# Attention and two expert layers: the first add of a pair's exponentials goes to VectorE, and the first batch is divided earlier

## The chip, the cores and the metric

The kernel runs on one core of a Trainium2 chip. Its time is the device time in microseconds of one execution, and the median of several runs is what is compared. The profile is of one execution; its span runs from the first instruction to the last.

## What is computed

Three layers over 4 batches of 448 positions: capped attention with 12 heads, a sparse layer of 4 attention experts of which the two best count for each position, and a gated feed-forward layer.

```python
def _attn_ref(q, k, v, cap):
    scores = scale * np.matmul(q, k.transpose(0, 1, 3, 2))
    scores = cap * np.tanh(scores / cap)
    attn = np.exp(scores - np.max(scores, axis=-1, keepdims=True))
    attn = attn / (np.sum(attn, axis=-1, keepdims=True) + 1e-09)
    return np.matmul(attn, v)
...
def _moe_ref(x, w_gate, wq, wk, wv, wo):
    logits = x @ w_gate
    topk = np.argpartition(-logits, 2, axis=-1)[..., :2]
...
    for e in range(E):
        a = causal softmax of scale * (x @ wq[e]) @ (x @ wk[e]).T
        ye = a @ (x @ wv[e]) @ wo[e]
        out += (e is in topk) * w[e] * ye
...
def _moe2_ref(x, w_in, g_ln, w_sg, b_sg, w_out):
    u, v = halves of gelu(x @ w_in)
    return x + (u * (w_sg @ layer_norm(v) * g_ln + b_sg)) @ w_out
```

## The kernel before

The heads are taken two at a time: 6 pairs for each of 4 batches, 24 pairs, and pair i is worked on in `slot(i)`. A slot computes the scores transposed, with 112 keys on the partitions, in two halves (h = 0 and 1) of two key chunks each. For a half, TensorE makes the scores s, ScalarE a tanh of each chunk and one exponential over both, which leaves p. The sum over keys that the softmax needs is built in two steps: the four chunks of p are added into one tile pb, and matmuls with a one-hot matrix (`sums`, on TensorE) add up its partitions for two pairs at once. pb takes three adds: the first joins the two chunks of half 0, the other two add the chunks of half 1 (`add_up`, on VectorE, at the end of the slot). For batch 0 the first add is VectorE's, for the 18 pairs of the other batches GpSimd's. `values` multiplies the previous pair's p by v and stores the product in os.

The rest of the program is laid into these slots at named places: "a" (twice: after the scores of half 0, and after the values; the second is "a1" to `normed`), "w" (before the values), "p" (after the scores of half 1) and "n" (the end). In slots 0 to 9 `prepare_weights` converts a 64-bit weight in 12 steps (wi0 to wi11, VectorE) and multiplies it (w2ps). `normed` finishes a batch six slots after its pairs: `invert` takes the reciprocal rs of the sums and sends it through DRAM (rd) into tiles rb that repeat it over the partitions; `over_sums` multiplies os by rb, in three parts; `in_parts` splits each part into a rounded part xh and a rest xl. From xh and xl the expert layer starts, by a plan: for a batch whose pairs end with slot 5, `queries_keys` (qk) comes in slots 10, 11, 14 and 15 of the program, `weigh` (scores a, their negated maxima m on VectorE, called minima here, exponentials pe on ScalarE) in slots 12, 13, 16 and 17, `values_chunk` (v, lg) in slots 12 and 13, `settle` (GpSimd scales pe by cs, 8 instructions) and `turn` (TensorE transposes pe into tr, copied out of PSUM to pt by VectorE) in slots 14, 15, 18 and 19; each later batch six slots later. At "p" the transposes are mixed into the matmuls of qk or v. All of these share three PSUM buffers g. `w_out` converts another weight (wuw, wum) on VectorE and then on GpSimd, at the end of slots 14 and 20 among others.

Up to slot 24 every engine executes in the order in which the code is written; a TensorE matmul is also tied to the one before it. DMAs are issued by SyncE in that order too. After slot 24 (near 290 us) a scheduler that estimates times sets the order. Every instruction of ScalarE, VectorE and GpSimd carries the line of one helper, L104, and every matmul L119, so rows are told apart by the tile names.

Of the kernel before, what the change touches and what calls it, by code (L numbers as in the profile page):

```python
# [10 lines left out]
F32 = mybir.dt.float32  # L11
# [6 lines left out]
ALU = mybir.AluOpType  # L18
# [3 lines left out]
B, H, S, D = 4, 12, 448, 64  # L22
# [6 lines left out]
CP, NC = 112, 4  # L29
# [8 lines left out]
def drain(gen):  # L38
    for _ in gen:
        pass  # L40
# [32 lines left out]
def build(ctx: ExitStack, tc: tile.TileContext, a: dict):  # L73
# [4 lines left out]
    def rnd(eng, out, in_):  # L78

        if eng == "a":  # L80
            act.activation(out, in_, AF.Copy)
        elif eng == "v":
            dve.tensor_copy(out, in_)
        else:
            pool_e.tensor_scalar(out, in_, 1.0, 0.0, op0=ALU.mult, op1=ALU.add)

    def rest(eng, out, in_, hi):

        e = dve if eng == "v" else pool_e
        e.tensor_tensor(out, in_, hi.bitcast(F32), op=ALU.subtract)  # L90
# [17 lines left out]
    act, dve, pool_e = InOrder(nc.scalar), InOrder(nc.vector), InOrder(nc.gpsimd)  # L108

    def pin(ins):  # L110

        if pe_pin[0] and pe_last:
            tc.add_manual_dep(ins.ins, pe_last[0].name,
                              mybir.DependencyInfo(mybir.DependencyClass.NoSync, mybir.DependencyReason.DATA),
                              reason="order")
        pe_last[:] = [ins.ins]

    def mm(*args, **kw):
        pin(nc.tensor.matmul(*args, **kw))  # L119
# [9 lines left out]
    onehot = const.tile([CP, 3, 32], F32, name="onehot")  # L129
# [44 lines left out]
    at = ah.enter_context(tc.tile_pool(name="at", bufs=2, side="right"))  # L174
    ps_s = ah.enter_context(tc.tile_pool(name="ps_s", bufs=2, space=PSUM, side="right"))
    ps_o = ah.enter_context(tc.tile_pool(name="ps_o", bufs=1, space=PSUM, side="right"))
    os_t, sums_t, pend, rb_d = {}, {}, {}, {}

    def load_pair(b, hp):

        qp = at.tile([128, S], F32, tag="qp", name=f"qp{b}_{hp}", bufs=3)
        kp = at.tile([128, S], F32, tag="kp", name=f"kp{b}_{hp}", bufs=3)
        vv = at.tile([CP, 2, NC, D], F32, tag="vv", name=f"vv{b}_{hp}", bufs=3)
        nc.sync.dma_start(kp, a["kT"][b, :, hp, :])
        nc.sync.dma_start(qp, a["qT"][b, :, hp, :])
        if (b, hp) == pairs[0]:
            scale()
            load_w(0)
        nc.sync.dma_start(vv, a["v"][b, :, 2 * hp:2 * hp + 2])
        return qp, kp, vv  # L190

    def scores(b, hp, h, qp, kp):

        p = at.tile([CP, 2, 2, S], F32, tag="p", name=f"p{b}_{hp}_{h}", bufs=4)
        for c2 in range(2):
            c = 2 * h + c2
            s = ps_s.tile([128, 2, 512], F32, tag="s", name=f"s{b}_{hp}_{c}")
            for j in range(2):
                r = slice(64 * j, 64 * j + 64)
                mm(s[:CP, j, :S], kp[r, c * CP:(c + 1) * CP], qp[r, :], start=True, stop=True)  # L200
            act.activation(p[:, :, c2, :], s[:CP, :, :S], AF.Tanh, scale=tsc[:CP])
            yield 805.0


        act.activation(p, p, AF.Exp, scale=capt[:CP])
        if h == 0:
            pb = at.tile([128, 2, S], F32, tag="pb", name=f"pb{b}_{hp}", bufs=3)[:CP]
            (dve if b == 0 else pool_e).tensor_tensor(pb, p[:, :, 0, :], p[:, :, 1, :], op=ALU.add)
            pend[b, hp] = (p, pb)
        else:  # L210
            p0, pb = pend[b, hp]
            pend[b, hp] = (p0, p, pb)

    def add_up(b, hp):
        _, p, pb = pend[b, hp]
        for c2 in range(2):
            dve.tensor_tensor(pb, pb, p[:, :, c2, :], op=ALU.add)

    def values(b, hp, vv):
        po = ps_o.tile([128, 512], F32, tag="po", name=f"po{b}_{hp}")  # L220
        for c in range(NC):
            for j in range(2):
                mm(po[64 * j:64 * j + 64, :S], vv[:, j, c, :], pend[b, hp][c // 2][:, j, c % 2, :],
                                 start=(c == 0), stop=(c == NC - 1))
            yield 805.0
        if hp % 2 == 0:
            os_t[b, hp // 2] = ao.tile([128, 2, S], F32, tag="os", name=f"os{b}_{hp}", bufs=5)
        act.activation(os_t[b, hp // 2][:, hp % 2, :], po[:, :S], AF.Copy)

    def sums(b, i):  # L230
        g = ps_g.tile([128, 512], F32, tag="g", name=f"sum{b}_{i}")
        for j in range(4):
            mm(g[32 * j:32 * j + 32, :S], onehot[:, i, :], pend[b, 2 * i + j // 2][2][:, j % 2, :],
                             start=True, stop=True)
        if i == 0:
            sums_t[b] = ao.tile([128, S], F32, name=f"rs{b}", tag="rs", bufs=1)
            dve.tensor_copy(sums_t[b], g[:, :S])
        else:
            dve.tensor_tensor(sums_t[b], sums_t[b], g[:, :S], op=ALU.add)
        yield 870.0  # L240

    def invert(b):
        dve.reciprocal(sums_t[b], sums_t[b])
        d = dr.tile([4, 32, S], F32, tag="rd", name=f"rd{b}")
        nc.sync.dma_start(d.rearrange("j r s -> (j r) s"), sums_t[b])
        rb_d[b] = d
        for h2 in range(2):
            load_rb(b, h2)

    pairs = [(b, hp) for b in range(B) for hp in range(HP)]  # L250
    ld = {}

    def slot(i, side):

        if i == 0:
            ld[0] = load_pair(*pairs[0])
            ld[1] = load_pair(*pairs[1])
        if i + 2 < len(pairs):  # L260
            qk = [at.tile([128, S], F32, tag=t, name=f"{t}{i + 2}", bufs=3) for t in ("qp", "kp")]
            b, hp = pairs[i + 2]
            nc.sync.dma_start(qk[1], a["kT"][b, :, hp, :])
            nc.sync.dma_start(qk[0], a["qT"][b, :, hp, :])
            ld[i + 2] = qk
        if i < len(pairs):
            first = scores(*pairs[i], 0, *ld[i][:2])
            drain(islice(first, 2))
            side("a")
            drain(first)  # L270
        else:
            side("a")
        side("w")
        if i:
            b, hp = pairs[i - 1]
            drain(values(b, hp, ld.pop(i - 1)[2]))
        if 0 < i < len(pairs) - 1:
            b, hp = pairs[i + 1]
            vv = at.tile([CP, 2, NC, D], F32, tag="vv", name=f"vv{b}_{hp}", bufs=3)
            nc.sync.dma_start(vv, a["v"][b, :, 2 * hp:2 * hp + 2])  # L280
            ld[i + 1] = (*ld[i + 1], vv)
        side("a")
        if i < len(pairs):
            drain(scores(*pairs[i], 1, *ld[i][:2]))
        side("p")
        if i:
            b, hp = pairs[i - 1]
            if hp % 2 == 1:
                drain(sums(b, hp // 2))
        if i < len(pairs):  # L290
            add_up(*pairs[i])
        side("n")


# [10 lines left out]
    def over_sums(b, h2):  # L305
        x = os_t[b, h2]
        dve.tensor_mul(x, x, rbs.pop((b, h2)))

    def in_parts(b, h2):

        if h2 == 0:
            X[b] = (xp.tile([128, KC, S], F32R, tag="xh", name=f"xh{b}"),
                    xp.tile([128, KC, S], F32R, tag="xl", name=f"xl{b}"))
        (xh, xl), x, o = X[b], os_t.pop((b, h2)), slice(2 * h2, 2 * h2 + 2)
        rnd("v", xh[:, o, :], x)
        rest("v", xl[:, o, :], x, xh[:, o, :])

    def normed(n, place):

        b = (n - 1) // HP - 1  # L320
        step = (n % HP, place)
        if n > B * HP + 4 or b < 0:
            return
        if step == (1, "a1"):
            invert(b)
        elif step == (3, "w"):
            over_sums(b, 0)
            over_sums(b, 1)
            load_rb(b, 2)
        elif b == 0 and step == (3, "a1"):  # L330
            in_parts(b, 0)
            in_parts(b, 1)
        elif step == (4, "w"):
            if b:
                in_parts(b, 0)
            over_sums(b, 2)
            if not b:
                in_parts(b, 2)
        elif b and step == (4, "a1"):
            in_parts(b, 1)  # L340
            in_parts(b, 2)
# [296 lines left out]
    with tc.tile_pool(name="pre", bufs=2) as pre:  # L638
        if WARM:
# [3 lines left out]
            g = ps_g.tile([128, 512], F32, tag="g", name="warm")  # L643
# [9 lines left out]
    for n in range(PRE_SLOTS, B * HP + 1):  # L653
        slot(n, beside(n))
# [256 lines left out]
```

## Time and profile before

| | us |
|---|---|
| median of 3 runs | 558.57 |
| lowest and highest | 557.87, 561.39 |
| the profiled execution | 559.72 |
| its span | 558.0 |
| TensorE busy | 532.7 |
| VectorE busy | 361.4 |
| ScalarE busy | 325.7 |
| GpSimd busy | 141.4 |

The span is the profiled execution without what lies around it. A busy time adds up an engine's instructions; TensorE's are pipelined, so its figure says that it had work and not that it ran at its peak. What limits the time at a place is told by the waits and by the timeline of that place.

### The profile page before, as it was taken

How to read it: one execution, taken by the hardware profiler on the slowest of the kernel's cores; microseconds unless marked ns; L12 is line 12 of the kernel's file. 1: busy time of each engine (PE TensorE's matmuls, PEld its weight loads, DVE VectorE, ACT ScalarE, POOL GpSimd, SP SyncE). 2: the span in 40 equal slices, each digit the busy share in tenths (PEclk: the TensorE clock that was granted, in tenths of full speed). 3: DMA queues.
4: the chain of work that ended last, by engine and by line, in shares of the span. 5: the costliest groups of instructions: out<-in, count | busy, mean ns of one | idle time of the engine just before them, and what ended most of it. 6: DMA issues, size and time to landing. Idle time of an engine off the chain costs nothing.

```text
span 558.0 us, 7562 instructions
## 1 busy us (share of the span) xinstructions
PE 532.7 (95%) x2732; PEld 346.3 (62%) x2732; DVE 361.4 (65%) x725; ACT 325.7 (58%) x508; POOL 141.4 (25%) x180
## 2 busy tenths in 40 slices
PE   7999999899999989999988989999999989999997
PEld 2333333455555554656557655878768879889996
DVE  3899999984666636567567599676631786485300
ACT  5988888688687896577822345353534344253211
POOL 0000122141155251243340364515521131031000
PEclk9999999999999999999999978999999999999999
DMA  8974615752424141322056221010421000000111
GB/s 246 338 217 123 207 51 160 223 175 80 130 67 142 50 140 49 103 71 67 22 158 165 54 59 58 29 58 0 162 101 64 2 0 34 33 34 33 51 49 66
DMA packets 30596, 53.97 MB, mean 97 GB/s; under 512 B 3872, under 2 KB 22880, under 8 KB 30560
## 3 DMA queue, kind: packets, MB, share of 16 engines
q1 hardware_dynamic: 29408, 48.26, 28.2%
q0 software_dynamic: 1152, 5.24, 2.8%
q8 instruction: 21, 0.34, 0.3%
q14 instruction: 15, 0.12, 0.1%
HBM read 41.83 MB, written 11.67 MB: 96 GB/s over the span
## 4 chain that ended last, share of the span: by engine, by line
PE 73%; DVE 16%; ACT 6%; DMA 2%; issue 2%; POOL 1%; DVEq 0%; POOLq 0%; ACTq 0%; SPq 0%
PE o L119 15%; PE po L119 10%; PE s L119 10%; PE qk L119 8%; PE sp L119 7%; PE v L119 5%; ACT p L104 4%; PE a L119 3%; PE hv L119 3%; PE hu L119 3%; PE w2ps L119 2%; PE tr L461 2%; PE av L119 2%; DVE pb L104 2%; DVE rs L104 2%
## 5 line engine op out<-in xcount | busy, mean ns | idle before, releaser
L104 ACT ACTIVATE p<-s,tsc 112x896 f32<-112x896 f32 x96 | 91.4, 1005 | 24.4 <-PE s L119 24.4
L119 PE MATMUL s<-qp,kp 64*112 64x448 f32 x384 | 84.4, 557 | 3.4 <-ACT p L104 3.4
L104 ACT ACTIVATE p<-p,capt 112x1792 f32<-112x1792 f32 x48 | 85.9, 1790 | 1.3
L104 POOL TENSOR_TENSOR pb<-p 112x896 f32<-112x896 f32 x18 | 38.9, 2163 | 166.6 <-ACT p L104 96.9
L119 PE MATMUL po<-p,vv 112*64 112x448 f32 x384 | 77.3, 545 | 0.0
L104 DVE TENSOR_TENSOR pb<-pb,p 112x896 f32<-112x896 f32 x48 | 57.3, 1194 | 16.0 <-ACT p L104 12.3
L119 PEld LDWEIGHTS s<-qp,kp 64*112 64x112 f32 x384 | 30.8, 172 | 50.6 <-issue 21.3
L119 PEld LDWEIGHTS po<-p,vv 112*64 112x64 f32 x384 | 25.5, 136 | 45.0 <-issue 44.0
L104 ACT ACTIVATE pe<-a,m 112x112 f32<-112x112 f32 (+3 forms) x64 | 31.2, 491 | 25.3 <-DVE m L104 24.5
L104 POOL TENSOR_SCALAR pe<-pe,cs 112x112 f32<-112x112 f32 (+1 forms) x64 | 31.6, 519 | 50.3 <-DVE cs L104 50.2
L104 DVE CUSTOM_DVE_ANT_0 a<-a,neg 112x112 f32<-112x112 f32 (+3 forms) x64 | 27.7, 464 | 20.0 <-PE a L119 20.0
L119 PE MATMUL qk<-xh,wqk_h 128*128 128x448 f32 x96 | 38.2, 398 | 2.6 <-DVE xh L104 2.6
L119 PE MATMUL o<-gh,wu_h 128*128 128x448 f32 x96 | 35.6, 371 | 0.8 <-DMA wu_h<-wud 0.8
L119 PE MATMUL o<-gl,wu_h 128*128 128x448 f32 x96 | 35.6, 371 | 0.0
L119 PE MATMUL qk<-xh,wqk_l 128*128 128x448 f32 x96 | 35.4, 369 | 0.0
L119 PE MATMUL a<-qk 64*112 64x112 f32 (+3 forms) x128 | 29.9, 440 | 5.6 <-ACT pe L104 3.4
L119 PE MATMUL o<-gh,wu_l 128*128 128x448 f32 x96 | 35.0, 370 | 0.0
L104 ACT ACTIVATE ob<-o 128x448 f32<-128x448 f32 x24 | 13.0, 541 | 31.5 <-PE o L119 31.3
L119 PE MATMUL v<-wvg_h,xh 128*112 128x260 f32 x96 | 28.7, 299 | 0.7 <-ACT pe L104 0.7
L461 PE MATMUL tr<-ident,pe 112*112 112x112 f32 x160 | 23.7, 261 | 4.9 <-DVE lg L104 1.8
L119 PE MATMUL v<-wvg_h,xl 128*112 128x260 f32 x96 | 27.1, 283 | 0.0
L119 PE MATMUL v<-wvg_l,xh 128*112 128x260 f32 x96 | 27.1, 282 | 0.0
(226 smaller groups left out, 1096.5 us busy)
## 6 DMA issues: line engine op xcount, KB each, us to landing
kp<-in_kT_dram SPq DMA_DIRECT2D x24, 224.0 KB, 3.1
qp<-in_qT_dram SPq DMA_DIRECT2D x24, 224.0 KB, 3.2
vv<-in_v_dram SPq DMA_DIRECT2D x24, 224.0 KB, 3.1
rb<-rd SPq DMA_DIRECT2D x24, 224.0 KB, 4.7
out_dram<-ob SPq DMA_DIRECT2D x24, 224.0 KB, 1.9
wuw<-in_w_out_dram SPq DMA_DIRECT2D x8, 384.0 KB, 3.5
wud<-wuw SPq DMA_DIRECT2D x16, 192.0 KB, 1.9
ws<-in_wqk_dram SPq DMA_DIRECT2D x4, 384.0 KB, 6.0
```

The costliest lines, as they stand in the source:

```text
L104: ins = f(*args, **kw)
L119: pin(nc.tensor.matmul(*args, **kw))
L461: pin(nc.tensor.transpose(g[:CP, j * CP:(j + 1) * CP], pe[:, j * CP:(j + 1) * CP], ident))
```

## The change

The first add of every pair, of batch 0 too, becomes a VectorE instruction, and it is issued at another place: no longer right behind the exponentials of half 0, but behind the second place "a" (the second minima, and what `normed` does at "a1") and before the scores of half 1. `add_up` gets the half as an argument; the tile pb is made there, and the sums find it in `pbs`. For batch 0 the steps of `normed` move: the first two divisions and the load of the third rb from slot 9 "w" to slot 8 "a1", the splitting of these parts from slot 9 "a1" to slot 9 "w", and the third part's division and splitting from slot 10 "w" to slot 9 "n".

```diff
--- before.py
+++ after.py
@@ -174,7 +174,7 @@
     at = ah.enter_context(tc.tile_pool(name="at", bufs=2, side="right"))
     ps_s = ah.enter_context(tc.tile_pool(name="ps_s", bufs=2, space=PSUM, side="right"))
     ps_o = ah.enter_context(tc.tile_pool(name="ps_o", bufs=1, space=PSUM, side="right"))
-    os_t, sums_t, pend, rb_d = {}, {}, {}, {}
+    os_t, sums_t, pend, pbs, rb_d = {}, {}, {}, {}, {}
 
     def load_pair(b, hp):
 
@@ -204,15 +204,17 @@
 
         act.activation(p, p, AF.Exp, scale=capt[:CP])
         if h == 0:
-            pb = at.tile([128, 2, S], F32, tag="pb", name=f"pb{b}_{hp}", bufs=3)[:CP]
-            (dve if b == 0 else pool_e).tensor_tensor(pb, p[:, :, 0, :], p[:, :, 1, :], op=ALU.add)
-            pend[b, hp] = (p, pb)
+            pend[b, hp] = (p,)
         else:
-            p0, pb = pend[b, hp]
-            pend[b, hp] = (p0, p, pb)
-
-    def add_up(b, hp):
-        _, p, pb = pend[b, hp]
+            pend[b, hp] = (*pend[b, hp], p)
+
+    def add_up(b, hp, h):
+        p = pend[b, hp][h]
+        if h == 0:
+            pb = pbs[b, hp] = at.tile([128, 2, S], F32, tag="pb", name=f"pb{b}_{hp}", bufs=3)[:CP]
+            dve.tensor_tensor(pb, p[:, :, 0, :], p[:, :, 1, :], op=ALU.add)
+            return
+        pb = pbs[b, hp]
         for c2 in range(2):
             dve.tensor_tensor(pb, pb, p[:, :, c2, :], op=ALU.add)
 
@@ -230,7 +232,7 @@
     def sums(b, i):
         g = ps_g.tile([128, 512], F32, tag="g", name=f"sum{b}_{i}")
         for j in range(4):
-            mm(g[32 * j:32 * j + 32, :S], onehot[:, i, :], pend[b, 2 * i + j // 2][2][:, j % 2, :],
+            mm(g[32 * j:32 * j + 32, :S], onehot[:, i, :], pbs[b, 2 * i + j // 2][:, j % 2, :],
                              start=True, stop=True)
         if i == 0:
             sums_t[b] = ao.tile([128, S], F32, name=f"rs{b}", tag="rs", bufs=1)
@@ -281,6 +283,7 @@
             ld[i + 1] = (*ld[i + 1], vv)
         side("a")
         if i < len(pairs):
+            add_up(*pairs[i], 0)
             drain(scores(*pairs[i], 1, *ld[i][:2]))
         side("p")
         if i:
@@ -288,7 +291,7 @@
             if hp % 2 == 1:
                 drain(sums(b, hp // 2))
         if i < len(pairs):
-            add_up(*pairs[i])
+            add_up(*pairs[i], 1)
         side("n")
 
 
@@ -323,19 +326,19 @@
             return
         if step == (1, "a1"):
             invert(b)
-        elif step == (3, "w"):
+        elif step == ((3, "w") if b else (2, "a1")):
             over_sums(b, 0)
             over_sums(b, 1)
             load_rb(b, 2)
-        elif b == 0 and step == (3, "a1"):
+        elif b == 0 and step == (3, "w"):
             in_parts(b, 0)
             in_parts(b, 1)
-        elif step == (4, "w"):
-            if b:
-                in_parts(b, 0)
+        elif b == 0 and step == (3, "n"):
             over_sums(b, 2)
-            if not b:
-                in_parts(b, 2)
+            in_parts(b, 2)
+        elif b and step == (4, "w"):
+            in_parts(b, 0)
+            over_sums(b, 2)
         elif b and step == (4, "a1"):
             in_parts(b, 1)
             in_parts(b, 2)
```

The first place is VectorE in slots 8 and 9 of the first batch's end, before; os are the divided parts, wqk_l and w2l pieces of converted weights:

```order
L104 TENSOR_TENSOR wqk_l<-ws_589,wqk_h 128x6x128
L104 COPY rs_696<-sum_0_691 128x448
L104 TENSOR_TENSOR pb_2_662<-pb_2_662,p_2_1_679 112x896 x2
L104 TENSOR_TENSOR wqk_l<-ws_664,wqk_h 128x6x128
L104 TENSOR_TENSOR os_0_217<-os_0_217,rb_0_616 128x896
L104 TENSOR_TENSOR os_2_335<-os_2_335,rb_1_619 128x896
L104 CAST xh_738<-os_0_217 128x896
```

And the same place now:

```order
L104 TENSOR_TENSOR wqk_l<-ws_587,wqk_h 128x6x128
L104 TENSOR_TENSOR os_0_215<-os_0_215,rb_0_614 128x896
L104 TENSOR_TENSOR os_2_333<-os_2_333,rb_1_617 128x896
L104 TENSOR_TENSOR pb_2_682<-p_2_0_643 112x896
L104 COPY rs_701<-sum_0_696 128x448
L104 TENSOR_TENSOR pb_2_682<-pb_2_682,p_2_1_684 112x896 x2
L104 TENSOR_TENSOR wqk_l<-ws_662,wqk_h 128x6x128
L104 CAST xh_723<-os_0_215 128x896
```

The two divisions moved ahead of the slot's adds, and the first add, GpSimd's before, stands between them.

The second place is VectorE in slot 14, as a piece of the difference; cs are the factors of `settle`, and pt the first copies of transposes:

```order
 L104 RECIPROCAL cs_0_1_950<-cs_0_1_950 112x4
 L104 TENSOR_TENSOR cs_0_1_950<-cs_0_1_950,wt_1183 112x4
+L104 TENSOR_TENSOR pb_2_1235<-p_2_0_1199 112x896
 L104 COPY pt_0_0_1251<-tr_0_0_0_1252 112x112
 L104 COPY pt_0_0_1251<-tr_0_0_1_1255 112x2x112
```

The add came in ahead of the first copy; nothing else moved.

The third place is VectorE in slot 15, before:

```order
L104 SCALAR_TENSOR_TENSOR wum_1_1193<-wuw_1_1192,wum_1_1193 128x384
L104 TENSOR_TENSOR os_0_600<-os_0_600,rb_0_1113 128x896
L104 TENSOR_TENSOR os_2_734<-os_2_734,rb_1_1116 128x896
L104 COPY pt_0_1_1354<-tr_0_1_0_1355 112x112
L104 COPY pt_0_1_1354<-tr_0_1_1_1358 112x2x112
```

And now:

```order
L104 SCALAR_TENSOR_TENSOR wum_1_1193<-wuw_1_1192,wum_1_1193 128x384
L104 TENSOR_TENSOR os_0_598<-os_0_598,rb_0_1111 128x896
L104 TENSOR_TENSOR os_2_738<-os_2_738,rb_1_1114 128x896
L104 TENSOR_TENSOR pb_3_1339<-p_3_0_1311 112x896
L104 COPY pt_0_1_1354<-tr_0_1_0_1355 112x112
L104 COPY pt_0_1_1354<-tr_0_1_1_1358 112x2x112
```

Here the add stands between the second batch's divisions and the first copy. Slot 21 has the same for the third batch, and in slot 19 the add stands between the reciprocal of `invert` and the first copy.

## Rows read from the trace of the kernel before

**Rows 1.** The page's first part: busy time, share of the span and instructions of each engine.

```profile
PE 532.7 (95%) x2732; PEld 346.3 (62%) x2732; DVE 361.4 (65%) x725; ACT 325.7 (58%) x508; POOL 141.4 (25%) x180
```

**Rows 2.** Costliest groups by form: count, busy us, mean ns, idle before and its releaser.

```profile
L104 POOL TENSOR_TENSOR pb<-p 112x896 f32<-112x896 f32 x18 | 38.9, 2163 | 166.6 <-ACT p L104 96.9 <-DVE pb L104 61.8 <-PE po L119 7.9
...
L104 DVE TENSOR_TENSOR pb<-pb,p 112x896 f32<-112x896 f32 x48 | 57.3, 1194 | 16.0 <-ACT p L104 12.3 <-POOL pb L104 2.8
...
L104 DVE TENSOR_TENSOR pb<-p 112x896 f32<-112x896 f32 x6 | 6.5, 1084 | 0.0
```

**Rows 3.** Timeline of VectorE, 60 to 125 us: start, duration, instruction, count.

```profile
63.77 2.65 DVE L104 TENSOR_SCALAR wi8m<-wi8m 128x512 f32<-128x512 f32 x2
...
69.52 2.21 DVE L104 TENSOR_TENSOR pb<-pb,p 112x896 f32<-112x896 f32 x2
...
72.11 0.89 DVE L104 TENSOR_SCALAR wi9m<-wi9m 128x512 f32<-128x512 f32 x2
73.03 2.45 DVE L104 SCALAR_TENSOR_TENSOR wi9m<-wi_3w,wi9m 128x512 int32<-128x512 int32 x1
...
78.69 0.69 DVE L104 SCALAR_TENSOR_TENSOR wi10m<-wi_4w,wi10m 128x512 int32<-128x512 int32 x1
...
84.08 3.07 DVE L104 TENSOR_TENSOR pb<-pb,p 112x896 f32<-112x896 f32 x2
...
92.37 3.97 DVE L104 TENSOR_TENSOR pb<-pb,p 112x896 f32<-112x896 f32 x2
...
103.66 3.90 DVE L104 TENSOR_TENSOR pb<-pb,p 112x896 f32<-112x896 f32 x2
...
122.14 2.92 DVE L104 TENSOR_TENSOR pb<-pb,p 112x896 f32<-112x896 f32 x2 [1.54 <-ACT p L104]
```

**Rows 4.** Timeline of GpSimd: the last of its five adds before 110 us.

```profile
103.39 2.09 POOL L104 TENSOR_TENSOR pb<-p 112x896 f32<-112x896 f32 x1 [8.00 <-ACT p L104]
```

**Rows 5.** Timeline of TensorE, slots 8 and 10; in brackets the idle time ahead.

```profile
86.53 1.62 PE L119 MATMUL sum<-pb,onehot 112*32 112x448 f32 x8
...
109.27 0.48 PE L119 MATMUL qk<-xh,wqk_h 128*128 128x448 f32 x1 [2.59 <-DVE xh L104]
...
111.51 0.96 PE L119 MATMUL sum<-pb,onehot 112*32 112x448 f32 x8
```

**Rows 6.** Timeline of four engines in slot 14.

```profile
153.84 1.79 ACT L104 ACTIVATE p<-p,capt 112x1792 f32<-112x1792 f32 x1
...
153.65 3.85 POOL L104 TENSOR_SCALAR pe<-pe,cs 112x112 f32<-112x112 f32 x8 [9.96 <-DVE cs L104]
...
155.61 0.58 DVE L104 COPY pt<-tr 112x112 f32<-112x112 f32 x2 [1.57 <-PE tr L461]
...
156.43 0.45 PE L461 MATMUL tr<-ident,pe 112*112 112x112 f32 x3
```

**Rows 7.** Timeline of VectorE, GpSimd and TensorE in slot 15.

```profile
166.03 2.40 DVE L104 TENSOR_TENSOR os<-os,rb 128x896 f32<-128x896 f32 x2
...
167.56 1.73 POOL L104 TENSOR_TENSOR wum<-wum,wuw 128x384 f32<-128x384 f32 x1
168.34 0.56 DVE L104 COPY pt<-tr 112x112 f32<-112x112 f32 x2
...
168.75 0.47 PE L461 MATMUL tr<-ident,pe 112*112 112x112 f32 x3
```

**Rows 8.** Timeline of VectorE in slot 21.

```profile
249.40 0.56 DVE L104 COPY pt<-tr 112x112 f32<-112x112 f32 x2
```

**Rows 9.** Timeline of TensorE in slot 19.

```profile
223.42 0.47 PE L461 MATMUL tr<-ident,pe 112*112 112x112 f32 x3 [1.05 <-DVE pt L104]
```

**Rows 10.** SyncE's issue of the first four rb loads, and landings of rb to 120 us.

```profile
86.12 2.57 SPq L302 DMA_DIRECT2D rb<-rd  x4
...
DMA to landing us min/median/max: 3.8/4.9/7.2
```

**Rows 11.** Timeline of TensorE behind the last slot.

```profile
327.90 1.08 PE L119 MATMUL a<-qk 64*112 64x224 f32 x2 [2.23 <-ACT pe L104]
```

## The prediction

> **What bounds the kernel now.** The first view is the page's busy line [rows 1]: TensorE is busy for 532.7 of 558.0 us, so only about 25 us of the span can be won by filling holes in it, wherever they lie. Second come the costliest groups [rows 2]: GpSimd takes 18 first adds at 2163 ns each, VectorE does the same add in 1084 ns (the six of the first batch) and the second adds in 1194 ns on average, although most of them take about 1.1. Third, the timeline of VectorE between 60 and 125 us [rows 3] says where that mean comes from. Two identical second adds take 2.21 us when GpSimd rests and 3.07, 3.97 and 3.90 us when a GpSimd add lies beside them; a pair of the weight conversion's cheap steps takes 0.89 us in one place and 2.65 in another, one of its bitwise steps 0.69 and 2.45. GpSimd's adds stand exactly there (63.43, 72.77, 83.00, 93.00 and 103.39 us; the last is shown, [rows 4]). VectorE stands still while GpSimd adds. Fourth, TensorE's own timeline says who pays [rows 5]: the row of sums at 86.53 us takes 1.62 us instead of 0.96, because it waits for pb, and the first matmuls on the first batch's x stop for 2.59 us at 109.27 us for the third part of xh, which VectorE, busy without a pause from 66 us, reaches late. After that TensorE is nearly gapless until 290 us, with one relevant hole, 1.05 us in slot 19 [rows 9].
>
> **Gain: the stretch of slots 6 to 10.** The five collisions of VectorE with GpSimd's adds cost it 2.65 - 0.89 = 1.76, 2.45 - 0.69 = 1.76, 3.07 - 2.21 = 0.86, 3.97 - 2.21 = 1.76 and 3.90 - 2.21 = 1.69 us, together 7.83 us [rows 3]. In their place it takes over the first adds of slots 6 to 9, 4 x 1.08 = 4.32 us [rows 2]; slot 10's add stands behind the last xl. So VectorE reaches the third xh 3.5 us earlier. What TensorE can get is 0.66 us at the sums and 2.59 us at xh, 3.25 us in all [rows 5]; a lead of 3.5 just covers it. One thing can eat into the lead. The two divisions by rb now stand in slot 8 before that slot's adds instead of in slot 9, and VectorE is 1.76 + 1.76 + 0.86 - 2 x 1.08 = 2.2 us ahead by then. Their place is about half a microsecond ahead of the second adds that began at 92.37 us [rows 3], so they begin near 89.6 and the second of them near 90.7 us. The four loads of rb were issued from 86.12 us over 2.57 us, and rb loads land 3.8 to 7.2 us after issue [rows 10]; the reciprocal before them comes 1.76 + 1.76 - 1.08 = 2.4 us earlier, so they land between 87.5 and 93.5 us. A wait of 0 to 2.8 us is possible. With no wait the gain is 3.25, with 2.8 it is 3.5 - 2.8 = 0.7; I take half a microsecond, since the middle of the landings is nearer to their start, and **3.0 us** (0.7 to 3.25). The loads and second-half weights that SyncE issues behind the earlier third load of rb are wanted slots later. The moves in slots 0 to 5 (the first batch's add behind the second conversion of slots 3 and 5) only swap neighbours on VectorE, whose sum of work there is unchanged; I count them at nothing, hidden by the two-slot lead of p and pb, and at most one add, 1.08 us, if that cover were gone.
>
> **Loss: the slots with transposes.** From slot 14 on, two slots of six interleave the transposes tr with queries_keys, slot 19 with the values, and VectorE copies each tr out of PSUM to pt. There are three PSUM buffers g: the main product has one, the first two tr the others, so the third tr waits until the first copy is done. The new add stands ahead of that copy, and everything on VectorE is in order.
> Slot 14: the exponentials of the first half end at 153.84 + 1.79 = 155.63 us; the first copies began at 155.61 and took 0.58, the third tr went at 156.43 [rows 6]. With the add, 155.63 + 1.08 = 156.71, plus the first copy (about 0.26) and its release (0.1), puts it at 157.08: 0.65 us lost. GpSimd's scaling of pe, 8 instructions in 3.85 us, is running then; waiting out one of them adds up to 0.5. I take **0.9** (0.65 to 1.15).
> Slot 15: VectorE is busy without a gap until the two divisions end at 166.03 + 2.40 = 168.43 us, the first copies follow at 168.34 and the third tr at 168.75, right behind the first of them [rows 7]. No slack is left, so the add's 1.0 us beyond its neighbour's end is lost in full. Beside it GpSimd wants its second w_out step, issued at 167.56 and 1.73 us long because it had to wait for the divisions. If it goes first, the add waits up to 1.0 us. In the row at 122.14 us two adds on VectorE among such w_out steps took 2.92 us, 0.71 more than the undisturbed 2.21 [rows 3], which is the nearest case. I take 1.0 + 0.7 = **1.7** (1.0 to 2.0).
> The Trainium skill (SBUF — State Buffer, "Who interferes with whom") says that the pair of ports is locked for a whole instruction by whichever asked first; the trace agrees as far as the alternation in that row goes. By that rule GpSimd's step, which had asked first, would cost the full 1.0, and the sum below would end 0.6 us higher.
> Slot 21 repeats slot 15 for the second batch [rows 8], **1.7** again. Slot 19: TensorE already waits 1.05 us for the first copy [rows 9], behind the reciprocal of invert; the add goes between the two: **1.05** more (1.0 to 1.1). Slot 20 looks like slot 14, but there the exponentials end well before the transposes begin, so the add fits in VectorE's idle time; if not, 0.9 as in slot 14. In all other slots the add lies where VectorE waits for ScalarE or TensorE, behind the minima or the parts of x that somebody wants, so nobody is delayed; GpSimd's freed time (38.9 us, [rows 2]) is worth nothing, since no row shows TensorE waiting for its adds.
> Losses: 0.9 + 1.7 + 1.05 + 1.7 = 5.35 us (3.65 to 6.25).
>
> **The sum.** 5.35 - 3.0 = +2.35 us (from 3.65 - 3.25 = +0.4 to 6.25 - 0.7 = +5.55). The profiled execution took 559.72 us, so it would take 562.1. It lies 1.15 us above the median of the three timed runs, 558.57, and I forecast medians: 558.57 + 2.35 = **560.9 us**.
>
> **Rivals.** (1) The copies don't bind: the third tr finds a free buffer, or the earlier VectorE never meets it, and only the gain stays. For it speaks that the collisions are large and sure; against it the third tr of slot 15 following the first copy within 0.2 us, and the wait in slot 19 named after pt. 558.57 - 3.0 = 555.6 us.
> (2) Slower by over 1%: VectorE's add doesn't get in between consecutive GpSimd instructions but waits out the whole series. In slot 14 it would wait until 153.65 + 3.85 = 157.5, and the third tr would go at 157.5 + 1.08 + 0.36 = 158.94, 2.5 us late; in slots 15 and 21 two more w_out steps of about 1.0 us come ahead of it, 3.0 us each; slot 20 would lose about 1.4. Losses 2.5 + 3.0 + 1.05 + 1.4 + 3.0 = 10.95, net +7.95, 566.5 us. It decides as soon as a series holds VectorE longer than one instruction; the row at 122.14 speaks against it.
> (3) The first batch's x is not done earlier after all, since rb is late by the full 2.8 us: the gain is 0.7, and the time 558.57 + 5.35 - 0.7 = 563.2 us.
> (4) The end: behind 320 us the scheduler's order of some twenty instructions of TensorE and VectorE swaps neighbours. One such wait as at 327.90 us, 2.23 us [rows 11], may come or go: 558.7 or 563.1 us.
>
> **How the numbers follow.** Forecast 0.58, rival 1 0.16, rival 2 0.10, rival 3 0.08, rival 4 0.08. One per cent, 5.6 us, is about what a measurement of this kernel can tell from no change. No case reaches 553 us; I leave 0.06 for an end that falls better by several such waits. Above 564.2 lie rival 2 and a little of the forecast's upper end: 0.14. The rest, 0.80, is within 1%. The range goes from rival 1, 555.6, to the forecast's upper end, 558.57 + 5.55 = 564.1: 555.5 to 564.5.
>
> **What would show it.** Right: GpSimd's pb rows gone, its busy time near 102 us; VectorE's pairs of second adds all near 2.2 us between 60 and 110 us; TensorE's 2.59 us hole before the third xh closed or under 1 us; and new waits of TensorE's tr for pt of 1 to 2 us in slots 15 and 21, about 1 us in slot 14, about 2.1 in slot 19. Wrong: tr rows without such waits (rival 1), an add on VectorE of over 3 us beside GpSimd's scaling (rival 2), or a wait of os for rb in slot 8 (rival 3).

## The result, and the profile after

The changed kernel takes **562.59 us** (median of 20 runs, 559.88 to 565.45) where the kernel before, run beside it, takes 558.66 (20 runs): a ratio of **1.0067, interval 1.0054 to 1.0080**, some 3.7 us slower by the ratio (3.9 between the medians). The prediction was 2.35 us slower. The profiled execution took 562.29 us, its span is 560.1.

The page's first part and two groups of the costliest ones (by form), after; they answer to [rows 1, 2]:

```profile
PE 531.3 (95%) x2732; PEld 345.1 (62%) x2732; DVE 372.9 (67%) x743; ACT 325.1 (58%) x508; POOL 109.0 (19%) x162
...
L104 DVE TENSOR_TENSOR pb<-pb,p 112x896 f32<-112x896 f32 x48 | 52.4, 1092 | 12.0 <-ACT p L104 10.9
...
L104 DVE TENSOR_TENSOR pb<-p 112x896 f32<-112x896 f32 x24 | 29.2, 1215 | 3.1 <-ACT p L104 3.1
```

GpSimd has 18 instructions fewer, VectorE 18 more. The second adds fell from 1194 to 1092 ns: they meet no GpSimd add any more. The first adds are no longer at 1084 but at 1215 ns on average, so some of them meet something else.

VectorE's timeline after, 82 to 109 us, the stretch of [rows 3]:

```profile
83.27 2.22 DVE L104 TENSOR_TENSOR pb<-pb,p 112x896 f32<-112x896 f32 x2
...
90.86 1.09 DVE L104 TENSOR_TENSOR os<-os,rb 128x896 f32<-128x896 f32 x1 [0.60 <-DMA rb<-rd]
93.19 1.09 DVE L104 TENSOR_TENSOR os<-os,rb 128x896 f32<-128x896 f32 x1 [1.24 <-DMA rb<-rd]
94.20 1.08 DVE L104 TENSOR_TENSOR pb<-p 112x896 f32<-112x896 f32 x1
...
95.73 2.21 DVE L104 TENSOR_TENSOR pb<-pb,p 112x896 f32<-112x896 f32 x2
...
104.26 2.21 DVE L104 TENSOR_TENSOR pb<-pb,p 112x896 f32<-112x896 f32 x2
106.39 1.08 DVE L104 TENSOR_TENSOR os<-os,rb 128x896 f32<-128x896 f32 x1
107.50 0.63 DVE L104 CAST xh<-os 128x896 fp32r<-128x896 f32 x1
```

Every pair of second adds takes 2.2 us, against 3.07, 3.97 and 3.90 before. New are two waits for rb, 0.60 + 1.24 = 1.84 us of idle VectorE, where the prediction had half a microsecond.

TensorE's timeline after: the sums of slot 8, then its rows that wait for xh or to transpose and differ from before (slots 10, 14, 15, 19 and 21; a wait of 1.53 us in slot 18, named after lg, stands in both kernels), and the first scores a of slot 24, where the stage measured below ends:

```profile
87.09 0.96 PE L119 MATMUL sum<-pb,onehot 112*32 112x448 f32 x8
...
108.19 0.47 PE L119 MATMUL qk<-xh,wqk_h 128*128 128x448 f32 x1 [1.61 <-DVE xh L104]
...
156.15 0.47 PE L464 MATMUL tr<-ident,pe 112*112 112x112 f32 x3 [0.66 <-POOL pe L104]
...
170.27 0.47 PE L464 MATMUL tr<-ident,pe 112*112 112x112 f32 x3 [1.65 <-DVE pt L104]
...
225.92 0.47 PE L464 MATMUL tr<-ident,pe 112*112 112x112 f32 x3 [2.05 <-DVE pt L104]
...
254.14 0.47 PE L464 MATMUL tr<-ident,pe 112*112 112x112 f32 x3 [1.66 <-DVE pt L104]
...
283.75 0.45 PE L119 MATMUL a<-qk 64*112 64x112 f32 x4 [0.86 <-ACT qk L104]
```

Against [rows 5, 9]: the sums gain 1.62 - 0.96 = 0.66 us, the hole before the third xh shrinks by 2.59 - 1.61 = 0.98; slot 14 loses 0.66, slots 15 and 21 lose 1.65 and 1.66, slot 19 loses 2.05 - 1.05 = 1.00. Net loss 4.97 - 1.64 = 3.33 us. Slot 20 has no wait.

These are the idle times in brackets, and they fall short of what the waits cost, since one matmul here overlaps the next: the one ahead of slot 15's third transpose takes 0.37 us, but before the change the transpose started 0.22 us behind its start. That matmul before, and after:

```profile
168.53 0.37 PE L119 MATMUL qk<-xh,wqk_l 128*128 128x448 f32 x1
```

```profile
168.25 0.37 PE L119 MATMUL qk<-xh,wqk_l 128*128 128x448 f32 x1
```

From start to start this was 168.75 - 168.53 = 0.22 us and is 170.27 - 168.25 = 2.02, so 1.80 us are lost. The same count gives 0.82 in slot 14, 1.00 in slot 19 and 1.80 in slot 21, 5.42 us in all, and a net loss of 5.42 - 1.64 = 3.78 us.

VectorE and GpSimd in slot 14, after, for [rows 6]:

```profile
154.57 1.26 DVE L104 TENSOR_TENSOR pb<-p 112x896 f32<-112x896 f32 x1 [1.58 <-ACT p L104]
155.75 0.56 DVE L104 COPY pt<-tr 112x112 f32<-112x112 f32 x2
...
153.38 0.55 POOL L104 TENSOR_SCALAR pe<-pe,cs 112x336 f32<-112x336 f32 x1
...
154.86 1.28 POOL L104 TENSOR_SCALAR pe<-pe,cs 112x224 f32<-112x224 f32 x1
```

TensorE's row of slot 14 names GpSimd's pe as what it waited for. But the third transposes read the 112x336 tile, scaled by 153.93. What ended at 156.14, just ahead of the row, is a scaling for the second expert, whose transposes come in slot 15. The first copy to pt began at 155.75 and the third transposes 0.40 us later, as in slot 15 (0.41, below). So this wait too is for the copy behind the add.

VectorE and GpSimd in slot 15, after, for [rows 7]:

```profile
165.73 2.39 DVE L104 TENSOR_TENSOR os<-os,rb 128x896 f32<-128x896 f32 x2
...
167.27 1.72 POOL L104 TENSOR_TENSOR wum<-wum,wuw 128x384 f32<-128x384 f32 x1
168.05 1.89 DVE L104 TENSOR_TENSOR pb<-p 112x896 f32<-112x896 f32 x1
...
169.86 0.56 DVE L104 COPY pt<-tr 112x112 f32<-112x112 f32 x2
```

The add takes 1.89 us: it waits until GpSimd's step ends at 168.99 and then runs its own 1.08 (169.94 - 1.08 = 168.86). The copies to pt follow it, 169.86 instead of 168.34, and the third transpose follows the first copy. The Trainium skill (SBUF — State Buffer, "Who interferes with whom") says of VectorE's two-port modes that whoever issues first holds the pair shared with GpSimd for the whole instruction, and that a VectorE instruction with two inputs in SBUF contends with GpSimd's reads too. The trace agrees for this add of two inputs: it runs only once that step has ended, to 0.13 us.

### The profile page after: what moved, and what is told of

It reads as the page before. It is cut to its first block, busy times and chain, and to the rows that moved or that the text cites. A ratio compares the mean times of both kernels' runs of the same rounds, so it can differ in the third digit from the quotient of the medians.

```text
span 560.1 us, 7562 instructions
## 1 busy us (share of the span) xinstructions
PE 531.3 (95%) x2732; PEld 345.1 (62%) x2732; DVE 372.9 (67%) x743; ACT 325.1 (58%) x508; POOL 109.0 (19%) x162
## 4 chain that ended last, share of the span: by engine, by line
PE 64%; DVE 21%; ACT 6%; DMA 5%; issue 2%; POOL 1%; SPq 0%; DVEq 0%; POOLq 0%; ACTq 0%
PE o L119 14%; PE po L119 8%; PE s L119 7%; PE qk L119 7%; PE sp L119 7%; PE v L119 5%; DVE pb L104 4%; ACT p L104 4%; PE a L119 3%; DMA rb<-rd 3%; PE hu L119 2%; PE hv L119 2%; PE tr L464 2%; PE av L119 2%; DVE wum L104 2%
## 5 line engine op out<-in xcount | busy, mean ns | idle before, releaser
L104 DVE TENSOR_TENSOR pb<-pb,p 112x896 f32<-112x896 f32 x48 | 52.4, 1092 | 12.0 <-ACT p L104 10.9
L104 POOL TENSOR_SCALAR pe<-pe,cs 112x112 f32<-112x112 f32 (+1 forms) x64 | 34.2, 555 | 89.5 <-DVE cs L104 52.5
L104 POOL TENSOR_SCALAR wuw<-wum 128x384 fp32r<-128x384 f32 x8 | 6.7, 835 | 184.8 <-DVE wum L104 171.8
L119 PE MATMUL a<-qk 64*112 64x112 f32 (+3 forms) x128 | 28.6, 430 | 4.9 <-ACT pe L104 2.6
L104 DVE TENSOR_TENSOR pb<-p 112x896 f32<-112x896 f32 x24 | 29.2, 1215 | 3.1 <-ACT p L104 3.1
L464 PEld LDWEIGHTS tr<-ident,pe 112*112 112x112 f32 x160 | 17.8, 133 | 15.6 <-issue 10.6
```

The costliest lines, as they stand in the source:

```text
L104: ins = f(*args, **kw)
L464: pin(nc.tensor.transpose(g[:CP, j * CP:(j + 1) * CP], pe[:, j * CP:(j + 1) * CP], ident))
```

## The experiments

All twelve were timed beside the kernel before, four to a chip. The stage that I compare in profiles runs from the first row of scores s that waits 1.71 us for p (slot 0) to the row a of slot 24 shown above. For the kernel before, TensorE's timeline has these two rows:

```profile
11.73 1.91 PE L119 MATMUL s<-qp,kp 64*112 64x448 f32 x8 [1.71 <-ACT p L104]
...
279.41 0.45 PE L119 MATMUL a<-qk 64*112 64x112 f32 x4 [0.86 <-ACT qk L104]
```

That is 267.68 us; "stage" in the table is a kernel's own figure minus this one. "Waits" is what the idle times of TensorE's rows sum to against before: the gain at the sums, the change of the hole at xh and of the transposes' waits, as in the sum that gave 3.33. "Half clock" says whether the granted clock fell to 0.50 right behind slot 19's wait.

| kernel | median | ratio, interval | hole at xh | wait in slot 19 | half clock | waits | stage |
|---|---|---|---|---|---|---|---|
| changed | 562.59 | 1.0067, 1.0054 to 1.0080 | 1.61 | 2.05 | no | +3.33 | +3.78 |
| e11, changed again | 562.77 | 1.0067, 1.0045 to 1.0088 | 0.42 | 2.05 | yes | +2.14 | +4.11 |
| e1, adds only | 562.00 | 1.0059, 1.0037 to 1.0080 | none | 2.05 | no | +1.72 | +1.88 |
| e12, adds only again | 561.99 | 1.0057, 1.0035 to 1.0080 | none | 2.05 | yes | +1.72 | +3.35 |
| e2, x only | 558.60 | 1.0004, 0.9980 to 1.0027 | 2.60 | 1.06 | no | +0.03 | +0.01 |
| e3, add behind the copies | 557.68 | 0.9986, 0.9969 to 1.0003 | 1.04 | 2.05 | no | -1.21 | -1.31 |
| e4, e3 with old x, slot 19 on GpSimd | 554.98 | 0.9936, 0.9915 to 0.9956 | none | 1.06 | no | -3.24 | -3.58 |
| e5, VectorE to slot 13 only, old x | 554.02 | 0.9890, 0.9853 to 0.9927 | none | 1.06 | no | -3.24 | -3.57 |
| e6, changed, w_out a slot later | 561.49 | 1.0037, 1.0015 to 1.0060 | 0.42 | 2.05 | yes | 0.00 | +2.26 |
| e7, e3 with old x | 556.53 | 0.9934, 0.9908 to 0.9959 | none | 2.05 | yes | -2.25 | -1.11 |
| e8, e7, invert earlier | 555.26 | 0.9908, 0.9873 to 0.9943 | none | 0.17 | no | -4.13 | -4.73 |
| e9, changed, invert earlier | 559.41 | 1.0009, 0.9993 to 1.0025 | 0.51 | 0.17 | no | +0.35 | +0.50 |
| e10, e5, invert earlier | **552.48** | 0.9884, 0.9860 to 0.9908 | none | 0.19 | no | -4.11 | -4.70 |

Two things stand in it. Where the clock stayed up, the waits account for the stage within 0.6 us, in all nine profiles; for the changed kernel the count from start to start closes the rest, 3.78. Where it fell, the stage is 1.1 to 2.3 us longer than the waits say, in all four.

**e1, the adds alone.** The steps of `normed` are back at their old places.

```diff
-        elif step == ((3, "w") if b else (2, "a1")):
+        elif step == (3, "w"):
             over_sums(b, 0)
...
-        elif b == 0 and step == (3, "w"):
+        elif b == 0 and step == (3, "a1"):
             in_parts(b, 0)
             in_parts(b, 1)
-        elif b == 0 and step == (3, "n"):
-            over_sums(b, 2)
-            in_parts(b, 2)
-        elif b and step == (4, "w"):
-            in_parts(b, 0)
+        elif step == (4, "w"):
+            if b:
+                in_parts(b, 0)
             over_sums(b, 2)
+            if not b:
+                in_parts(b, 2)
```

> The adds moved as in the change, the first batch's divisions and splittings at their old places. Theory (the earlier divisions catch rb before it has landed, and the wait eats VectorE's lead): VectorE's 3.5 us lead reaches the third xh whole, TensorE's hole of 1.61 us at about 108 us closes to under 0.3, and the time is about 561.0 us, 1.6 below the changed kernel; the waits for pt in slots 15, 19 and 21 stay at 1.65, 2.05 and 1.66 us. Rival (the earlier divisions are what makes x ready in time): the hole grows to over 2 us and the time to 563.2 or more. Rival (the place of the divisions is neutral): 562.6.

Measured 562.00, 1.0 above what was expected; the interval holds the 562.6 of the neutral rival, so the rows have to decide. The hole at xh is gone altogether, and all four waits in the slots with transposes stay (0.65, 1.66, 2.05, 1.66): the loss belongs to the adds, and the adds alone also bring the whole gain.

**e2, x alone.** The first adds stay GpSimd's, behind the exponentials; the steps of `normed` move as in the change.

```diff
-            pend[b, hp] = (p,)
+            pb = at.tile([128, 2, S], F32, tag="pb", name=f"pb{b}_{hp}", bufs=3)[:CP]
+            (dve if b == 0 else pool_e).tensor_tensor(pb, p[:, :, 0, :], p[:, :, 1, :], op=ALU.add)
+            pend[b, hp] = (p, pb)
...
-            add_up(*pairs[i], 0)
             drain(scores(*pairs[i], 1, *ld[i][:2]))
```

> The adds as before the change (GpSimd for 18 pairs), only the first batch's divisions and splittings moved as in the change. Theory: with no lead, VectorE comes to the divisions near 91.8 us, the second rb lands near 95 us, and VectorE loses 1 to 2.5 us there; TensorE's hole at xh grows from 2.59 to 3.5 to 5 us; time about 560.2 us, 1.5 above the kernel before. Rival (the move alone brings x earlier): 556 to 558 us.

Measured 558.60, no change; the expectation missed. The rows of VectorE, of GpSimd and of TensorE in this kernel:

```profile
93.91 2.67 DVE L104 TENSOR_TENSOR os<-os,rb 128x896 f32<-128x896 f32 x1 [0.43 <-DMA rb<-rd]
...
97.04 2.20 DVE L104 TENSOR_TENSOR pb<-pb,p 112x896 f32<-112x896 f32 x2
```

```profile
93.56 2.08 POOL L104 TENSOR_TENSOR pb<-p 112x896 f32<-112x896 f32 x1 [7.93 <-PE po L119]
```

```profile
109.83 0.47 PE L119 MATMUL qk<-xh,wqk_h 128*128 128x448 f32 x1 [2.60 <-DVE xh L104]
```

GpSimd's add in slot 9 now meets the second division (2.67 us instead of 1.08), and the second adds, freed of it, take 2.20 instead of 3.97 us. The collision only changes its partner, and the third xh is as late as before.

**e3, the add behind the copies.** In slots 14, 15, 20 and 21 the first add goes behind the place "p", where the copies to pt are; the rest is as changed.

```diff
+    LATE = (14, 15, 20, 21)
...
-            add_up(*pairs[i], 0)
+            if i not in LATE:
+                add_up(*pairs[i], 0)
             drain(scores(*pairs[i], 1, *ld[i][:2]))
         side("p")
+        if i in LATE:
+            add_up(*pairs[i], 0)
```

> The changed kernel, but in slots 14, 15, 20 and 21 the first add is issued behind the transposes' copies, ahead of the second adds. Theory (the loss is the add ahead of the first copy of a transpose): the waits of tr for pt in slots 14, 15 and 21 (0.66, 1.65 and 1.66 us, and about 0.2 in slot 20) go, the one of 2.05 in slot 19 stays, and the time is about 558.4 us, 4.2 below the changed kernel. Rival (the time goes elsewhere, behind 290 us): 562 us.

Measured 557.68, as expected. The waits of slots 14, 15 and 21 are gone, slot 19's is not. VectorE in slot 15 of this kernel:

```profile
165.95 0.56 DVE L104 COPY pt<-tr 112x112 f32<-112x112 f32 x2
...
168.07 0.62 DVE L104 COPY pt<-tr 112x448 f32<-112x448 f32 x1 [0.70 <-PE tr L468]
168.61 1.08 DVE L104 TENSOR_TENSOR pb<-p 112x896 f32<-112x896 f32 x1
```

The add takes 1.08 us there and holds nobody up. So the order of add and copies is the cause of these three waits.

**e4.** e3, the old places of the first batch's x (the edit of e1), and slot 19's first add on GpSimd again.

```diff
+    GP = (19,)
...
+            if b * HP + hp in GP:
+                add_up(b, hp, 0)
...
-            dve.tensor_tensor(pb, p[:, :, 0, :], p[:, :, 1, :], op=ALU.add)
+            (pool_e if b * HP + hp in GP else dve).tensor_tensor(pb, p[:, :, 0, :], p[:, :, 1, :], op=ALU.add)
...
-            if i not in LATE:
+            if i not in LATE and i not in GP:
                 add_up(*pairs[i], 0)
```

> As e3, with the first batch's divisions and splittings at their old places and slot 19's first add on GpSimd at its old place. Theory: both losses gone and the whole gain of the collisions kept, 558.7 - 3.25 = 555.4 us; the hole at xh under 0.3 us, the wait in slot 19 back at 1.05. Rival (the gain of the early stretch is given back later): 558 us or more.

Measured 554.98, near the 555.4 expected. Slot 19's wait is back at 1.06, so the add was the other 1.00. No loss is left in the rows, and the gain of 3.25 us that the prediction had as its upper end is there in full.

**e5.** e4 with GpSimd's adds from slot 14 on, as before the change, and VectorE's only up to slot 13.

```diff
-    GP = (19,)
-    LATE = (14, 15, 20, 21)
+    GP = (14, 15, 16, 17, 18, 19, 20, 21, 22, 23)
```

> VectorE takes the first adds only up to slot 13; from slot 14 on they are GpSimd's at their old place; the first batch's x at its old places. Theory (the gain is all in slots 6 to 10, the loss all in slots 14 to 21): no hole at xh, no wait of tr for pt beyond the 1.05 of slot 19 of the kernel before, slot 24 reached 3.3 us earlier than before, time about 555.4 us, the same as with the adds behind the copies and slot 19's on GpSimd (554.98). Rival (GpSimd's later adds also cost VectorE time that TensorE pays for): 557 us or more.

Measured 554.02, 1.4 under what was expected. The stage is that of e4 (-3.57 and -3.58): behind slot 13 VectorE's adds bring nothing up to slot 24, even where they do no harm. The median fell by 5.3 us, more than the stage; where the rest comes from is not shown.

**e6.** The changed kernel, with `w_out`'s conversions of slots 14 and 20 at the end of slots 15 and 21.

```diff
-    W_OUT = {11: ("w", xp, "rb0", "rb1"), 14: ("n", at, "ws", "ws"), 17: ("w", at, "ws", "ws"),
-             20: ("n", at, "ws", "ws"), 23: ("w", at, "ws", "ws"),
+    W_OUT = {11: ("w", xp, "rb0", "rb1"), 15: ("n", at, "ws", "ws"), 17: ("w", at, "ws", "ws"),
+             21: ("n", at, "ws", "ws"), 23: ("w", at, "ws", "ws"),
```

> The changed kernel, with the w_out conversions at the end of slots 14 and 20 put at the end of slots 15 and 21. Theory (no slack: VectorE's row of work from the sums to the first copy is full, and the add and a GpSimd step of w_out come on top): 2.6 us of that row go away, the first copies are ready before the third tr, the waits of 1.65 and 1.66 us in slots 15 and 21 are gone and the add there takes 1.08 us instead of 1.89; time about 559.3 us. Rival (the add behind the minima is late for another reason, as its exponentials or the divisions): the waits stay, 562.6.

Measured 561.49, 2.2 above what was expected. VectorE and TensorE in slots 15 and 16:

```profile
164.05 1.09 DVE L104 TENSOR_TENSOR pb<-p 112x896 f32<-112x896 f32 x1
...
166.59 0.58 DVE L104 COPY pt<-tr 112x112 f32<-112x112 f32 x2 [1.44 <-PE tr L464]
```

```profile
182.15 0.47 PE L119 MATMUL qk<-xh,wqk_h 128*128 128x448 f32 x1 [0.59 <-DVE xh L104]
```

The mechanism held: without the conversion ahead of it VectorE is early, the add takes 1.09 us, and the copies wait for the transposes instead. What was gained came back elsewhere: 0.59 us for xh in slot 16 and again in slot 22, and half clock behind slot 19's wait.

**e7.** e3 with the old places of x.

> All adds on VectorE, those of slots 14, 15, 20 and 21 behind the copies, the first batch's x at its old places. It differs from the run with the late adds alone (557.7) only in the first batch's x. Theory: the hole at xh, 1.04 us there, is gone, 556.5 us; slot 19's wait stays at 2.05 us. Rival (the moves of x are neutral in time): 557.7.

Measured 556.53. Against e3 only the place of x differs, and the intervals of the two ratios (0.9908 to 0.9959, 0.9969 to 1.0003) don't meet, by a narrow gap and on two chips, each beside the kernel before: x at the new places costs time.

**e8.** e7, and the reciprocal of the third batch before the values of slot 19 instead of behind them.

```diff
-        if step == (1, "a1"):
+        if step == (1, "w" if b == 2 else "a1"):
             invert(b)
```

> As the run before it, and slot 19's invert (the third batch's reciprocal, 2.95 us on VectorE) is issued ahead of the values instead of behind the second minima. Theory: reciprocal and add end before the first tr is done, slot 19's wait of 2.05 us goes, nothing else changes, 556.5 - 2.05 = 554.5 us. Rival (the second minima then wait for the reciprocal and TensorE or ScalarE pays): 555.5 us or more.

Measured 555.26, between the 554.5 expected and the rival's 555.5; the interval holds both. The rows speak for the theory: slot 19's wait is 0.17 us, no other wait of TensorE came in the stage, and the stage is the shortest of all, 4.73 us under before. In this profile, of the slowest of its seven runs, the program behind slot 24 is longer (279.5 us from that row to the span's end, 276.4 in e5).

**e9.** The changed kernel with the same edit.

> The changed kernel, with slot 19's invert issued ahead of the values, so that its reciprocal and the new add are done before the first transpose. Theory: the wait of 2.05 us in slot 19 goes, and with it the stretch of 0.50 granted clock that followed it in two of five profiles and cost 1.5 to 1.8 us there; 562.6 - 2.05 - 0.4 x 1.65 = 559.9 us, and no clock below 1.00 between 215 and 235 us. Rival (that stretch has nothing to do with the wait): 560.5 us, and the low clock may still be seen.

Measured 559.41, near the 559.9 expected, but the interval reaches to the rival's 560.5. It is 3.2 us under the changed kernel (3.4 under e11 on the same chip), of which 2.05 - 0.17 = 1.88 is the wait. The clock stays up behind it; one profile cannot show that it always does. The windows of its profile around slot 19 (columns: the window; its length, then busy time of TensorE's matmuls and loads, VectorE, ScalarE and GpSimd with their instructions; the granted clock; the DMAs' share and GB/s) are to be read against those of e11 below:

```profile
220.00:225.00 5.00, 4.83 (x41) 4.62 (x42) 2.65 (x6) 4.48 (x7) 0.00 (x0) 1.00 0.40 97
225.00:230.00 5.00, 5.00 (x35) 2.58 (x35) 3.44 (x10) 0.50 (x2) 0.00 (x0) 1.00 0.69 198
```

**e10.** e5 with the same edit: the version to keep.

> VectorE's adds to slot 13, GpSimd's from slot 14, the first batch's x at its old places, and slot 19's invert ahead of the values. Theory: against the same without the last edit (554.02) the 1.05 us wait of slot 19 goes too: 553.0 us, the fastest of all. Rival (the reciprocal ahead of the second minima costs as much): 554.0 us.

Measured **552.48**, 6.7 us under the kernel before and the lowest median of all. Whether the edit brings its 0.87 us in time as well as in the rows is not settled: the ratio of e5 is 0.9890, its interval holds e10's. As in e5, the median fell by more than the stage (4.70 us), and where the rest comes from is not shown.

**e11 and e12**, the changed kernel and e1 once more, for the price of x at its new places.

> The changed kernel itself once more, beside its variants on one chip. Theory: 562.6 us; its waits as before (0.66, 1.65, 2.05 and 1.66 us), its hole at xh between 0.4 and 1.7 us by where the rb loads land; a stretch at 0.50 clock behind slot 19's wait in some executions, not in all. Rival (the run to run differences lie elsewhere): the hole at xh is 1.6 us again.

> The run with the adds alone once more, beside the changed kernel on the same chip, to size the part of the moved x. Theory: no hole at xh, and 1.0 to 1.6 us less than the changed kernel, 561.0 to 561.6 us. Rival (the moves of x are neutral in time): the same as the changed kernel.

Measured 562.77 and 561.99. The hole of 0.42 in e11 was as expected; e12 came 0.8 us under e11, less than the 1.0 to 1.6 expected. In times x costs 0.6 and 0.8 us in the two pairs, within their intervals, so these times alone do not show a cost. The stage, compared at like clock, has 3.78 - 1.88 = 1.9 us (clock up) and 4.11 - 3.35 = 0.8 (clock down); the hole at xh, 1.61 and 0.42, is most of the first and half of the second.

## Why the prediction was right, and where its sizes were off

**Right: the sign and the places.** GpSimd's collisions with VectorE went, as the pairs at 2.2 us show. The new waits stand in slots 14, 15, 19 and 21 and not in 20, as forecast, and from start to start they cost 5.42 us where 5.35 was forecast: 1.80 and 1.80 for 1.7, 1.00 for 1.05, 0.82 for 0.9. e3 shows the cause of three of them, the add ahead of the copies; e4 shows it for slot 19, and e9 that the rest of that wait comes from the reciprocal ahead. In slot 15 the add waited 1.89 - 1.08 = 0.81 us for GpSimd's step, between the 0.7 that the prediction took from the nearest row and the 1.0 that it had as the most.

**Not as forecast: two of the signs.** The sign of rival 3, a wait of os for rb in slot 8, stands in the profile, and the hole at xh is 1.61 and not under 1 us; both belong to the term that follows. And the prediction had a change of under 1% as hardly to be told from none: the interval of the ratio is only 0.26% wide, so 0.67% is clear of no change.

**Mis-sized: the gain of 3.0 us.** The step "I take half a microsecond" for the waits for rb was too kind to x at its early place. In the profile of the changed kernel they were 1.84 us and the gain 1.64; in e11 0.74 us was waited, and the gain was 0.66 + 2.59 - 0.42 = 2.83. e11's division and third xh:

```profile
91.97 1.09 DVE L104 TENSOR_TENSOR os<-os,rb 128x896 f32<-128x896 f32 x1 [0.74 <-DMA rb<-rd]
```

```profile
106.96 0.47 PE L119 MATMUL qk<-xh,wqk_h 128*128 128x448 f32 x1 [0.42 <-DVE xh L104]
```

So the mechanism held: the lead of 3.5 us less the wait gives 1.66 and 2.76. Only the size of the wait was wrong, and it varies from execution to execution. Five profiles with adds and x moved have holes at xh of 0.42, 0.42, 0.51, 1.04 and 1.61 us, 0.80 on average, so the gain is 2.45 on average, from 1.64 to 2.83: inside the bounds given, 0.7 to 3.25. The whole 3.25 comes without the move of x (e1, e4, e5, e7 have no hole): with the collisions gone VectorE is early enough, and at the old places rb has long landed. That part of the change is worth nothing by itself (e2) and costs something beside the adds: a hole in all five profiles, and a time clear of its interval in one pair of three (e3 against e7).

**Missing: the clock behind slot 19.** The prediction counted the wait there as 1.05 us more and nothing else. In four of the seven profiles with the wait at 2.05 us the granted clock fell to 0.50 behind it. e1 and e12 are one kernel, without and with it: 3.35 - 1.88 = 1.5 us. Over the executions, with four in seven taken as the share, this is an estimate of 0.9 us. With the gain at 2.45 and the waits at 5.42 the sum is 5.42 - 2.45 + 0.9 = +3.9 us, against 3.7 to 3.9 measured; the predicted +2.35 had the gain too large and lacked the clock.

**The rivals.** That the copies don't bind (1) and that the add waits out a whole series of GpSimd's (2) fall with the rows of slot 15: 1.89 us, one step waited out and no more. The late rb (3) is real but smaller than its 2.8 us. Of the end (4) the profiles show only that it varies: from slot 24's row to the span's end before has 558.0 - 279.41 = 278.6 us and after 560.1 - 283.75 = 276.4, and all fourteen profiles lie between 275.0 and 279.5. These are single executions, and the 3.78 us lost in the stage are near what the medians show (3.9 apart).

## What to carry to other kernels

An instruction that is moved from one engine to another is to be judged stretch by stretch: the same add gained 3.25 us where it had blocked VectorE as long as GpSimd ran it (e1), and lost 5.42 where it stood ahead of copies out of PSUM that TensorE waited for; giving VectorE only the first stretch (e5, e10) keeps the gain and has no loss. On an engine that executes in order, ask of each inserted instruction what stands right behind it and who waits for that. And a step that was made earlier because its engine would be late should be tried without that once the engine is no longer late: here the earlier step met loads that had not landed.

## What was not expected of the hardware

The granted clock fell behind an idle time of 2.05 us of TensorE in slot 19, in e6, e7, e11 and e12, and not in the changed kernel's profile, e1 and e3, which have the same wait. It did so in none of the four profiles with the wait at 1.05 or 1.06 us (before, e2, e4, e5) and none of the three at 0.17 to 0.19 (e8, e9, e10). The windows of e11 around the wait, and three of TensorE's rows there:

```profile
222.00:224.00 2.00, 0.64 (x6) 0.41 (x4) 2.00 (x2) 1.97 (x3) 0.00 (x0) 1.00 0.62 219
224.00:226.00 2.00, 1.31 (x8) 1.34 (x9) 1.35 (x4) 1.02 (x1) 0.00 (x0) 0.73 0.34 123
226.00:228.00 2.00, 2.00 (x12) 1.99 (x12) 0.00 (x0) 0.38 (x1) 0.00 (x0) 0.50 0.29 97
228.00:230.00 2.00, 2.00 (x17) 2.00 (x17) 0.69 (x2) 0.00 (x0) 0.00 (x0) 0.92 0.67 196
```

```profile
224.69 0.59 PE L464 MATMUL tr<-ident,pe 112*112 112x112 f32 x3 [2.05 <-DVE pt L104]
...
225.51 0.42 PE L119 MATMUL v<-wvg_h,xl 128*112 128x260 f32 x1
...
228.99 0.28 PE L119 MATMUL v<-wvg_h,xl 128*112 128x260 f32 x1
```

The last column but two is the clock: 1.00 (2.4 GHz) until the wait ends, 0.50 (1.2 GHz) for some 3.4 us of full work behind it, then 1.00 again. The same matmul takes 0.42 us in it and 0.28 outside. Why three executions with the same wait kept their clock is open. Elsewhere in the stage the clock stays at 1.00 in all these profiles; behind the stage it falls in every one, the kernel before's too (0.50 from 328 to 332 and from 344 to 350 us there).

GpSimd pays for collisions too. Its scaling of pe in slot 14, eight instructions, took 3.85 us before [rows 6] and takes 4.68 with VectorE's add beside it, 1.28 of them in the one step shown for slot 14 above. As said there, TensorE does not wait for that step, though its row names it. This is one reason why GpSimd's busy time fell to 109.0 us and not to the 102 that was forecast. The row after:

```profile
152.61 4.68 POOL L104 TENSOR_SCALAR pe<-pe,cs 112x112 f32<-112x112 f32 x8 [31.34 <-ACT p L104]
```
